# Retiming the pieces of a DFT inside a feed-forward token loop: inverse pieces five steps later, smaller first blocks, and a new plan for the second and third batches

## The chip, the cores and the metric

One core of one Trainium2 chip runs the whole kernel. The metric is the time of one execution on the device in microseconds, lower is better. A run without the profiler gives one time; a profiled execution gives a time too, and the span that its trace covers.

## The reference

The input `x` is 8 batches of 3008 tokens with 256 features. Each batch goes through a global filter along its tokens, and the result through a feed-forward layer with a PReLU whose negative slope is one number per hidden unit:

```python
X = np.fft.rfft(x, axis=1)
y = np.fft.irfft(X * (filt_r + 1j * filt_i)[None], n=3008, axis=1)
h = y.reshape(24064, 256) @ w_in                 # 256 -> 2048
g = np.maximum(h, 0.0) + alpha * np.minimum(h, 0.0)
out = g @ w_out                                  # 2048 -> 256
```

## The kernel before

**The transform.** 3008 is 47 times 64, so the forward and the inverse transform are each two sets of small matrix products in fp16 with a transposition between them. For one batch (`class Fft`) there are four kinds of pieces, each a few matmuls into one PSUM bank of the pool `psF`, which has two buffers:

- `piece_a` (16 of them; matmul in line 168): one matmul of 512 columns out of a loaded chunk `xs` of the input, evicted to `asb`. Every fourth is followed by `save_a` (L173), a DMA of a quarter of `asb` to DRAM. After all of them `turn_a` (L180) reads the whole back in another order, as `at`, in four DMAs of 384 KB.
- `piece_b` (12; L188): two matmuls of 256 columns out of `at`. VectorE multiplies the bank twice with the filter, into `uu` (L191) and `ww` (L192), two tiles of the pool `p_uw`.
- `piece_c` (12; L220 and L221): four matmuls of 256 columns out of `uu` and `ww`, evicted by ScalarE to `v`. Every third is followed by `turn_c` (L230), four DMAs of `v` to DRAM; after the last the whole is read back as `zt` (L236).
- `piece_d` (16; L243): four matmuls of 94 columns out of `zt`, evicted into `yT`, the transposed activations that the feed-forward layer reads. `yT` holds two batches.

Evictions are one helper each: ScalarE in line 250, VectorE in line 253. The input is loaded by GpSimd's queue (`load_x`, L123) into four chunk buffers: a chunk of the next batch can be loaded when the four pieces A of this batch that read it are done.

**The feed-forward layer.** The tokens of two batches at a time are cut into blocks (12 blocks of 512 tokens, one of them 384). A block has 16 steps, one for each 128 hidden units. In a step `up` issues two matmuls as wide as the block (L332); every second step ScalarE evicts two such results at once to `gt` (L337), and VectorE makes the PReLU of them with two multiplications (`m`, L340) and one addition (L341). In the same step `down` issues the second product for the block before this one: as many matmuls of 256 columns as that block has 128-token groups (L350). Results go out through `osb` (L355) and SyncE's queue (L316).

**The order.** It is written out by hand. The whole runs as one sequence of steps, 96 for a batch, and `plan` says which pieces follow the `up` and `down` of which step; `plan_fft` enters a batch's pieces. Every engine works through its instructions in the order of this plan, and SyncE's queue too: it holds the stores of results, `save_a`, `turn_a`, `turn_c` and the reads of `zt` in one line, and an entry that waits holds up all behind it. The first batch's transform runs ahead of step 0, apart from its last twelve pieces D. The second batch's pieces lie in the first batch's steps, and so on: each batch's A, B and C must be done, and its D begun, before the step in which its own tokens are reached.

Of the kernel before, what the change touches and what calls it, by code (L numbers as in the profile page):

```python
# [13 lines left out]
NFFT = 3008  # L14
# [52 lines left out]
def kernel(  # L67
# [17 lines left out]
    konst = ctx.enter_context(tc.tile_pool(name="konst", bufs=1))  # L85
    p_x = ctx.enter_context(tc.tile_pool(name="p_x", bufs=4))
    p_fft = ctx.enter_context(tc.tile_pool(name="p_fft", bufs=1))
    p_uw = ctx.enter_context(tc.tile_pool(name="p_uw", bufs=2))
    p_gt = ctx.enter_context(tc.tile_pool(name="p_gt", bufs=17))
    p_m = ctx.enter_context(tc.tile_pool(name="p_m", bufs=2))  # L90
    p_osb = ctx.enter_context(tc.tile_pool(name="p_osb", bufs=3))
# [28 lines left out]
    def load_x(b, c):  # L120
        xs = p_x.tile([2 * N1, 8 * D], FP16, name="xs")
        for h in range(2):
            nc.gpsimd.dma_start(out=xs[h * N1 : h * N1 + N1], in_=xrow(b, h, c))  # L123
        return xs
# [130 lines left out]
    both = (on_act, on_dve)  # L255
# [41 lines left out]
        f0.piece_d(i, both[i % 2], i % 2 == 1)  # L297


    sizes = [512] * 5 + [384] + [512] * 6  # L300
    blocks = []
    for p in range(NB // 2):
        t = 0
        for n, tn in enumerate(sizes):
            blocks.append((p, t, tn, 2 * p + (n >= 6)))
            t += tn

    def store(p, t0, osb, lane):
# [52 lines left out]
    def put(step, fn, *args):  # L361
        plan.setdefault(step, []).append((fn, args))

    def plan_fft(b, a0, ga, ta, b0, gap, d0):
        f = Fft(b)
        for i in range(16):
            put(a0 + ga * i, f.piece_a, i, on_act)
        for c in range(4):
            put(a0 + ga * (4 * c + 3), f.save_a, c)
            if b + 1 < NB:  # L370
                put(a0 + ga * (4 * c + 3) + 1,
                    lambda b=b, c=c: xc.update({(b + 1, c): load_x(b + 1, c)}))
        put(ta, f.turn_a, nc.sync)
        for kp in range(12):
            put(b0 + gap * kp, f.piece_b, kp)
            put(b0 + gap * kp + 3, f.piece_c, kp, on_act)
        for q in range(4):
            put(b0 + gap * (3 * q + 2) + 4, f.turn_c, q)
        for i in range(16):
            put(d0 + min(i, 4) + 2 * max(i - 4, 0), f.piece_d, i, on_act)  # L380

    for i in range(4, 16):
        put(i - 4, f0.piece_d, i, both[i % 2])
    plan_fft(1, 10, 1, 26, 40, 3, 92)
    plan_fft(2, 50, 2, 86, 104, 5, 187)
    for b in range(3, NB):
        p = 96 * (b - 1)
        plan_fft(b, p - 54, 2, p - 22, p + 6, 5, p + 91)

    prev = None  # L390
    step = 0
    for p, t0, tn, _ in blocks:
        blk = Block(p, t0, tn)
        for j in range(16):
            blk.up(j)
            if prev is not None:
                prev.down(j)
            for fn, args in plan.pop(step, ()):
                fn(*args)
            step += 1  # L400
        prev = blk
# [33 lines left out]
```

## Time and the profile before

| | us |
|---|---|
| times of three runs | 860.27, 862.39, 858.70 |
| median | 860.27 |
| profiled execution, own time | 863.19 |
| its span | 861.4 |
| TensorE busy in it | 799.4 (93%) |
| VectorE busy | 612.9 (71%) |
| ScalarE busy | 586.6 (68%) |

TensorE's matmuls overlap in the trace, so the mean duration of one (273 ns for 256 columns) is longer than the distance between two. "Granted clock" or PEclk is the TensorE clock as a share of full speed. An idle time is put down to what ended it. Step 0 starts 64.62 us into the span; what lies ahead of it is not touched by the change.

### The profile page before, as it was taken

To read this page: it belongs to the slowest core of one execution; us is meant where nothing else is said; L and a number is where in the kernel's file an instruction comes from. 1 tells how busy PE (TensorE), PEld (TensorE's weight loads), DVE (VectorE), ACT (ScalarE), POOL (GpSimd) and SP (SyncE) were. 2 spreads that over 40 slices of the span, in tenths; PEclk is the share of its full clock that TensorE was granted. 3 is DMA by queue.
4 is the path that set the end of the run, shared out by engine and by line. 5 is a ranking of instruction groups with operands and counts; after the bars stand their busy time and mean duration, and the time that the engine had idled before them with its cause. 6 is when DMAs were issued, how large, how long until landed. Compare 5 with 4: busy or idle time off the path is not lost.

```text
span 861.4 us, 15404 instructions
## 1 busy us (share of the span) xinstructions
PE 799.4 (93%) x5809; PEld 541.7 (63%) x5809; DVE 612.9 (71%) x1361; ACT 586.6 (68%) x817; POOL 41.4 (5%) x85
## 2 busy tenths in 40 slices
PE   3458989979999999999999999999999999999997
PEld 1134556756666766676666766676666766676665
DVE  2246668758877787678877787778877788777773
ACT  2027757767787767777777767777777866677663
POOL 4103000000000000000000000000000000000000
PEclk9989989999999999999999999999999999999999
DMA  9989835761368224772268323682148122411111
GB/s 212 250 171 197 179 69 133 157 144 41 75 148 199 60 62 97 172 158 51 53 162 195 73 64 83 164 181 50 43 120 186 50 68 50 129 38 39 39 41 49
DMA packets 95378, 95.95 MB, mean 111 GB/s; under 512 B 8312, under 2 KB 85128, under 8 KB 95176
## 3 DMA queue, kind: packets, MB, share of 16 engines
q1 hardware_dynamic: 85448, 78.19, 35.8%
q0 software_dynamic: 8256, 16.00, 12.3%
q10 hardware_dynamic: 1600, 0.79, 0.5%
q8 instruction: 45, 0.74, 0.4%
q14 instruction: 29, 0.24, 0.1%
HBM read 59.55 MB, written 49.81 MB: 127 GB/s over the span
## 4 chain that ended last, share of the span: by engine, by line
PE 70%; DVE 13%; ACT 7%; DMA 6%; issue 2%; SPq 1%; POOL 0%; ACTq 0%; DVEq 0%; POOLq 0%
PE hps L332 29%; PE op L350 28%; ACT gt L337 6%; DVE gt L341 4%; DVE m L340 4%; PE psF L168 3%; DVE ww L192 3%; DVE uu L191 3%; PE psF L221 2%; DMA at<-a_dram 2%; PE psF L243 2%; DMA a_dram<-asb 2%; PE psF L220 1%; DMA xs<-in_x_dram 1%; PE psF L188 1%
## 5 line engine op out<-in xcount | busy, mean ns | idle before, releaser
L337 ACT ACTIVATE gt<-hps 128x1024 f16<-128x1024 f32 (+1 forms) x384 | 385.1, 1003 | 134.6 <-PE hps L332 134.1
L332 PE MATMUL hps<-yT,win_s 128*128 128x512 f16 (+1 forms) x1536 | 454.3, 377 | 1.1 <-ACT yT L250 1.0
L350 PE MATMUL op<-wout_s,gt 128*128 128x256 f16 x3008 | 453.3, 273 | 0.6 <-DVE gt L341 0.6
L350 PEld LDWEIGHTS <-gt 128*128 128x128 f16 x3008 | 294.4, 98 | 192.5 <-issue 2.8
L340 DVE TENSOR_SCALAR m<-gt,alm_s 128x512 f16<-128x512 f16 (+1 forms) x768 | 233.5, 346 | 164.1 <-ACT gt L337 162.8
L341 DVE TENSOR_TENSOR gt<-gt,m 128x1024 f16<-128x1024 f16 (+1 forms) x384 | 261.6, 681 | 24.3 <-DVE m L340 0.9
L332 PEld LDWEIGHTS <-win_s 128*128 128x128 f16 x1536 | 145.6, 98 | 31.6 <-issue 5.0
L250 ACT ACTIVATE asb<-psF 96x512 f16<-96x512 f32 x120 | 70.7, 593 | 40.2 <-PE psF L168 40.2
L250 ACT ACTIVATE v<-psF 128x512 f16<-128x512 f32 x84 | 50.2, 598 | 34.9 <-PE psF L221 34.9
L250 ACT ACTIVATE yT<-psF 128x376 f16<-128x376 f32 x120 | 58.1, 484 | 20.9 <-PE psF L243 20.7
L191 DVE TENSOR_TENSOR uu<-psF,filt_s 128x512 f16<-128x512 f32 x84 | 57.4, 683 | 6.7 <-PE psF L188 6.7
L355 ACT ACTIVATE osb<-op 128x512 f32<-128x512 f32 x96 | 56.3, 587 | 6.9 <-PE op L350 3.7
L168 PE MATMUL psF<-xs,wf_s 94*96 94x512 f16 x120 | 47.8, 398 | 11.0 <-DMA xs<-in_x_dram 8.3
L192 DVE TENSOR_TENSOR ww<-psF,filts_s 128x512 f16<-128x512 f32 x84 | 57.1, 679 | 0.0
L123 POOL DMA_DIRECT2D xs<-in_x_dram x64 | 32.9, 522 | 458.2 <-PE psF L168 457.1
L243 PE MATMUL psF<-wi_s,zt 96*128 96x94 f16 x504 | 42.7, 207 | 10.8 <-DMA zt<-v_dram 9.0
L243 PEld LDWEIGHTS <-zt 96*128 96x128 f16 x512 | 36.3, 100 | 18.9 <-DMA zt<-v_dram 9.3
L221 PE MATMUL psF<-ww,twi_s 128*128 128x256 f16 x168 | 41.1, 272 | 6.2 <-DVE ww L192 3.5
L220 PE MATMUL psF<-uu,twi_s 128*128 128x256 f16 x168 | 42.9, 272 | 1.1 <-ACT yT L250 0.5
L188 PE MATMUL psF<-at,twf_s 128*128 128x256 f16 x168 | 32.3, 274 | 8.1 <-issue 4.5
L220 PEld LDWEIGHTS <-twi_s 128*128 128x128 f16 x192 | 19.0, 99 | 18.0 <-issue 13.2
L250 ACT ACTIVATE v<-op 128x512 f16<-128x512 f32 x12 | 7.2, 597 | 32.4 <-PE op L221 32.4
(35 smaller groups left out, 130.8 us busy)
## 6 DMA issues: line engine op xcount, KB each, us to landing
out_dram<-osb SPq DMA_DIRECT2D x128, 128.0 KB
a_dram<-asb SPq DMA_DIRECT2D x32, 384.0 KB
v_dram<-v SPq DMA_DIRECT2D x128, 96.0 KB
zt<-v_dram SPq DMA_DIRECT2D x32, 384.0 KB
xs<-in_x_dram POOLq DMA_DIRECT2D x64, 188.0 KB, 5.1
at<-a_dram SPq DMA_DIRECT2D x28, 384.0 KB
twi_s<-c_twi SPq DMA_DIRECT2D x2, 768.0 KB
filts_s<-filt_s SPq DMA_DIRECT2D x2, 768.0 KB
```

Source lines behind the costliest of these rows:

```text
L168: nc.tensor.matmul(ps[0:96], wf1_s, xs[:, o : o + 512], start=True, stop=True)
L191: nc.vector.tensor_mul(uu, px, filt_s[:, 2 * kp : 2 * kp + 2])
L192: nc.vector.tensor_mul(ww, px, filts_s[:, 2 * kp : 2 * kp + 2])
L220: nc.tensor.matmul(pv[:, kh], twi_s[:, k1, 0], uu[:, kh], start=True, stop=False)
L221: nc.tensor.matmul(pv[:, kh], twi_s[:, k1, 1], ww[:, kh], start=False, stop=True)
L243: nc.tensor.matmul(ps[:, m], self.zt[:, 8 * g + 4 * mh + m, dh * 128 : dh * 128 + 128], wi3_s, start=True, stop=True)
L250: nc.scalar.activation(o, i, AF.Copy)
L332: nc.tensor.matmul(self.hps[:, j % 2, 0:tn], win_s[:, kt, j * 128 : (j + 1) * 128], yT[:, kt, self.t0 : self.t0 + tn], start=(kt == 0), st ...
L337: nc.scalar.activation(g[:, :, 0:tn], self.hps[:, :, 0:tn], AF.Copy)
L340: nc.vector.tensor_scalar(m[:, i, 0:tn], g[:, i, 0:tn], 0.0, a, OP.min, OP.mult)
L341: nc.vector.tensor_add(g[:, :, 0:tn], g[:, :, 0:tn], m[:, :, 0:tn])
L350: nc.tensor.matmul(self.op[:, si % 2], self.gts[k][:, 128 * si : 128 * si + 128], wout_s[:, k], start=(k == 0), stop=(k == 15))
```

## The change

Six things change in the plan; no piece is added, and one block more is cut.

1. In batches 3 to 8 piece C follows its piece B by five steps instead of three, and so lands in the same step as the next piece B. `p_uw` gets three buffers instead of two.
2. The first pair of batches is cut into blocks of 256, 256, 384 and ten of 512 tokens: 13 blocks, so that the second batch begins at step 112 and all later ones 16 steps later than before.
3. The second batch's pieces A are spread over steps 18 to 48, one in two steps, and evicted by ScalarE and VectorE in turn (before: steps 10 to 25, one a step, all by ScalarE). Its `turn_a` is at step 49, its B from 62 and C from 65, one in three steps, D from 110.
4. The third batch's loads stand at step 52 in the plan, its pieces A at 69 to 99, its `turn_a` at 101, B from 118, C from 123.
5. From the fourth batch on, B begins one step earlier against the batch's start.
6. Pieces D begin with two in a step: two, two, one, and then one in two steps.

```diff
-    p_uw = ctx.enter_context(tc.tile_pool(name="p_uw", bufs=2))
+    p_uw = ctx.enter_context(tc.tile_pool(name="p_uw", bufs=3))
...
-    sizes = [512] * 5 + [384] + [512] * 6
-    blocks = []
+    blocks, begin = [], {}
     for p in range(NB // 2):
         t = 0
-        for n, tn in enumerate(sizes):
-            blocks.append((p, t, tn, 2 * p + (n >= 6)))
+        for tn in [256, 256, 384] + [512] * 10 if p == 0 else [512] * 5 + [384] + [512] * 6:
+            for half in range(2):
+                if t <= half * NFFT < t + tn:
+                    begin[2 * p + half] = 16 * len(blocks)
+            blocks.append((p, t, tn))
             t += tn
...
-    def plan_fft(b, a0, ga, ta, b0, gap, d0):
+    def plan_fft(b, a0, ga, ta, b0, gap, late, d0, x0, evict_a):
         f = Fft(b)
         for i in range(16):
-            put(a0 + ga * i, f.piece_a, i, on_act)
+            put(a0 + ga * i, f.piece_a, i, evict_a[i % 2])
         for c in range(4):
             put(a0 + ga * (4 * c + 3), f.save_a, c)
             if b + 1 < NB:
-                put(a0 + ga * (4 * c + 3) + 1,
+                put(max(x0, a0 + ga * (4 * c + 3) + 1),
                     lambda b=b, c=c: xc.update({(b + 1, c): load_x(b + 1, c)}))
         put(ta, f.turn_a, nc.sync)
         for kp in range(12):
             put(b0 + gap * kp, f.piece_b, kp)
-            put(b0 + gap * kp + 3, f.piece_c, kp, on_act)
+            put(b0 + gap * kp + late, f.piece_c, kp, on_act)
         for q in range(4):
-            put(b0 + gap * (3 * q + 2) + 4, f.turn_c, q)
+            put(b0 + gap * (3 * q + 2) + late + 1, f.turn_c, q)
         for i in range(16):
-            put(d0 + min(i, 4) + 2 * max(i - 4, 0), f.piece_d, i, on_act)
+            put(d0 + (i // 2 if i < 4 else 2 * i - 6), f.piece_d, i, on_act)
...
-    plan_fft(1, 10, 1, 26, 40, 3, 92)
-    plan_fft(2, 50, 2, 86, 104, 5, 187)
+    p = begin[1]
+    plan_fft(1, 18, 2, 49, p - 50, 3, 3, p - 2, p - 60, both)
+    plan_fft(2, p - 43, 2, p - 11, p + 6, 5, 5, begin[2] - 5, 0, (on_act, on_act))
     for b in range(3, NB):
-        p = 96 * (b - 1)
-        plan_fft(b, p - 54, 2, p - 22, p + 6, 5, p + 91)
+        p = begin[b - 1]
+        plan_fft(b, p - 54, 2, p - 22, p + 5, 5, 5, begin[b] - 5, 0, (on_act, on_act))
```

In `plan_fft` the batches count from 0: `plan_fft(1, ...)` is the second batch.

More of the change, by code (lines that the diff above doesn't have):

```diff
@@ L375, in plan_fft @@
             put(b0 + gap * kp, f.piece_b, kp)
-            put(b0 + gap * kp + 3, f.piece_c, kp, on_act)
+            put(b0 + gap * kp + late, f.piece_c, kp, on_act)
         for q in range(4):
-            put(b0 + gap * (3 * q + 2) + 4, f.turn_c, q)
+            put(b0 + gap * (3 * q + 2) + late + 1, f.turn_c, q)
         for i in range(16):
-            put(d0 + min(i, 4) + 2 * max(i - 4, 0), f.piece_d, i, on_act)
+            put(d0 + (i // 2 if i < 4 else 2 * i - 6), f.piece_d, i, on_act)
     for i in range(4, 16):
         put(i - 4, f0.piece_d, i, both[i % 2])
-    plan_fft(1, 10, 1, 26, 40, 3, 92)
-    plan_fft(2, 50, 2, 86, 104, 5, 187)
+    p = begin[1]
+    plan_fft(1, 18, 2, 49, p - 50, 3, 3, p - 2, p - 60, both)
+    plan_fft(2, p - 43, 2, p - 11, p + 6, 5, 5, begin[2] - 5, 0, (on_act, on_act))
     for b in range(3, NB):
-        p = 96 * (b - 1)
-        plan_fft(b, p - 54, 2, p - 22, p + 6, 5, p + 91)
+        p = begin[b - 1]
+        plan_fft(b, p - 54, 2, p - 22, p + 5, 5, 5, begin[b] - 5, 0, (on_act, on_act))
     prev = None
     step = 0
-    for p, t0, tn, _ in blocks:
+    for p, t0, tn in blocks:
         blk = Block(p, t0, tn)
```

## The prediction

> **What bounds the kernel now.** I read the busy shares by stage first. The columns: stretch and its length, busy time of TensorE, its weight loads, VectorE, ScalarE and GpSimd, then granted clock, DMA share and GB/s.
>
> ```profile
> 64.60:105.70 41.10, 37.84 (x246) 22.01 (x246) 28.11 (x65) 31.71 (x46) 8.59 (x17) 0.96 0.92 188
> 105.70:110.40 4.70, 0.21 (x3) 0.07 (x2) 1.27 (x3) 0.42 (x1) 0.00 (x0) 0.84 1.20 219
> 110.40:115.90 5.50, 5.50 (x21) 2.95 (x22) 2.60 (x5) 1.67 (x2) 0.00 (x0) 0.52 0.09 30
> 115.90:182.90 67.00, 63.97 (x480) 44.93 (x478) 50.84 (x113) 50.09 (x74) 4.01 (x8) 1.00 0.60 133
> 182.90:186.60 3.70, 0.08 (x2) 0.08 (x2) 1.18 (x3) 0.48 (x1) 0.00 (x0) 1.00 1.00 224
> 186.60:190.90 4.30, 4.30 (x22) 2.48 (x23) 2.60 (x5) 2.37 (x4) 0.00 (x0) 0.60 0.01 3
> 190.90:862.00 671.10, 657.73 (x4892) 455.54 (x4889) 504.69 (x1135) 485.87 (x670) 16.28 (x32) 1.00 0.40 95
> ```
>
> From 190.9 on TensorE is busy for 98%: every wait it has there is lost. Ahead of that it stands still twice, and works at half clock after each. The waits name both:
>
> ```profile
> PE psF L188 <- issue: 4.5, 1, 4.5
> PE psF L188 <- DMA at<-a_dram: 3.6, 1, 3.6
> PE psF L168 <- ACT v L250: 2.0, 5, 0.5
> ```
>
> Both stalls are the first B of a batch waiting for `at`. SyncE's queue shows the chain behind each:
>
> ```profile
> 94.01 0.31 SPq L173 DMA_DIRECT2D a_dram<-asb  x1
> 100.29 2.46 SPq L180 DMA_DIRECT2D at<-a_dram  x4
> ...
> 158.62 1.80 SPq L230 DMA_DIRECT2D v_dram<-v  x4
> 163.86 1.72 SPq L236 DMA_DIRECT2D zt<-v_dram  x4
> 165.63 2.35 SPq L316 DMA_DIRECT2D out_dram<-osb  x3
> 168.02 0.58 SPq L173 DMA_DIRECT2D a_dram<-asb  x1
> 175.64 4.06 SPq L180 DMA_DIRECT2D at<-a_dram  x4
> ```
>
> The last save of batch 2 takes 6.3 us (94.01 to 100.29), the reread 10.1 (to the first B at 110.36). For batch 3 the same queue carries the older batch's v, zt and three stores first, and the first B starts at 186.55.
>
> The small waits are in the groups of instructions (the number ahead of the arrow is the idle time just before them):
>
> ```profile
> L221 PE MATMUL psF<-ww,twi_s 128*128 128x256 f16 x168 | 41.1, 272 | 6.2 <-DVE ww L192 3.5
> L220 PE MATMUL psF<-uu,twi_s 128*128 128x256 f16 x168 | 42.9, 272 | 1.1 <-ACT yT L250 0.5
> ```
>
> Piece C waits for the filter products for 6.2 + 1.1 = 7.3 us in all, about 1.2 a batch.
>
> **C five steps late: gain 7.3, then what is next.** `ww` is done within three steps of its B, so at five steps the wait is gone: −7.3 (certain to a microsecond). But C now shares a step with the next B, and where the older batch's D or the next batch's A falls there too, three pieces want two `psF` banks, and the third waits for an eviction. Before shows the price, at step 52, where C, B and A meet:
>
> ```profile
> 126.24 0.38 PE L188 MATMUL psF<-at,twf_s 128*128 128x256 f16 x2
> 127.09 0.38 PE L168 MATMUL psF<-xs,wf_s 94*96 94x512 f16 x1 [0.47 <-ACT v L250]
> ```
>
> Counting such steps in the new plan (p is the step in which the batch before begins, from which `plan_fft` counts):
> - C, B, A: at p+50 and p+60 of each of five batches (158 and 168 for batch 3), even steps like 52: 10 × 0.47 = 4.7.
> - D, C, B: at p+15 of batches 4 to 8, odd steps, in which ScalarE first evicts `gt` (1.02). The first bank is free about 2.0 us into the step and TensorE wants it at 0.87 + 0.17 + 0.44 = 1.5: 5 × 0.55 = 2.8; once in batch 3 in an even step: 0.2.
> - Batch 2 beside A of batch 3 has four such steps now (2.0 in the waits above), and five after, on odd steps (about 0.62): +1.1.
> - Two D a step, the second pair behind the first's evictions: about 0.2 in each of six batches: 1.2.
>
> Sum 10.0 − 7.3 = **+2.7**. Bounds: the third piece may wait only the 0.17 that is left of the 2.0 after four waits of 0.47, and the D pairs nothing (−4.5), or all of it a quarter more (+5.2). I take the middle, since the step-52 row is the same arrangement.
>
> **Small blocks and spread pieces A: where batch 2's `at` starts.** VectorE's rows by width:
>
> ```profile
> L341 DVE TENSOR_TENSOR gt<-gt,m 128x1024 f16<-128x1024 f16 x352 | 243.7, 692 | 20.6 <-DVE m L340 0.9 <-PE hps L332 0.5
> L340 DVE TENSOR_SCALAR m<-gt,alm_s 128x512 f16<-128x512 f16 x704 | 216.0, 349 | 153.0 <-ACT gt L337 151.7
> L341 DVE TENSOR_TENSOR gt<-gt,m 128x768 f16<-128x768 f16 x32 | 17.8, 558 | 3.6 <-PE hps L332 0.5
> L340 DVE TENSOR_SCALAR m<-gt,alm_s 128x384 f16<-128x384 f16 x64 | 17.6, 317 | 11.1 <-ACT gt L337 11.1
> ```
>
> Two `m` overlap: two steps' PReLU takes 0.62 + 0.69 = 1.31 at 512 tokens and 0.55 + 0.56 = 1.11 at 384, so I take 0.91 at 256: half the tokens, but 70% of the time. TensorE needs 0.85 for such two steps, and 1.09 at 384: in the first 48 steps VectorE is the bound. It has six pairs of steps with a `yT` cast (0.91 + 0.5), ten without (0.91), eight of 384 (1.11) and eight `asb` casts (0.6, a little under their 687 ns): 8.5 + 9.1 + 8.9 + 4.8 = 31.3 us. Its first `m`, at 68.17 before, starts 1.3 sooner with narrower matmuls and evictions: 66.9, so the last A is evicted at 98.2. Save and reread take 0.1 + 6.3 + 10.1: B at **114.7**. TensorE reaches the last A (step 48) two pairs and a cast ahead of VectorE, about 95.9, and 14 steps of 0.76 (two up, three down) later, at 106.5, it wants that B: a stall of 8.2 us instead of 4.7. By then it has 4352 columns more behind it than before (44,032 against 41,984 of `up`, 27,904 against 25,600 of `down`), 1.8 us at 0.43 per 1024. So the loss is 114.7 − (110.36 + 1.8) = **+2.5**. Ends: A15 bound by TensorE alone (about 96.5) with a faster save, −0.5; the slower save and reread of batch 3's chain (7.6 and 10.9), +4.6.
>
> One rule decides otherwise. The Trainium skill ("DMA: Bandwidth & Descriptors", Anatomy of one DMA) puts a DMA at about 2 us plus its bytes at 436 GB/s, fitted on GpSimd's path; by that, an estimate, save and reread take 2.9 + 5.6 = 8.5 us, B starts at 106.8 and this stall is gone. The queue's rows say 16.4, and I go by them.
>
> **Batch 3's `at`.** Its last A now stands in step 99, the step of batch 2's last `turn_c` (before: three steps later). From the start of the last C to the first B the chain took 157.5 to 186.55, 29.0 us. Of it the three stores between zt and save go (2.4): 26.6. Cover: the C, 20 steps of 0.87, one A, eight D of 0.17 and the up matmul that waits for D as before (1.0): 0.4 + 17.4 + 0.2 + 1.4 + 1.0 = 20.4. A stall of 6.2 against 3.7: **+2.5** (ends: chain 25.0 to 29.0, so +0.9 to +4.9). D of batch 2, at step 110, has 11 steps instead of 15 after its `turn_c`; should it wait (0 to 2.3), that time comes off the stall behind it.
>
> **Half clock.** Before: 5.5 us at 0.52 cost 2.6, 4.3 at 0.60 cost 1.7. Both stalls get longer: 3.0 and 2.6, **+1.3** (0 to +3.7, if the first is like the start, where the clock came back 10.9 us after a wait of 17.9). The skill's page "TensorE: Matmul & The Clock Gate" (Part 1) speaks against longer stalls too: an idle window of about 3.4 us halves the clock until a busy one has passed.
>
> **Nothing:** the third `uu`/`ww` buffer (C comes ahead of B in its step, two suffice); the loads at step 52 (GpSimd's queue holds only loads there, which wait for pieces A, not steps); B one step earlier in later batches (their `at` is not waited for); 16 more steps of ScalarE evictions (68% busy).
>
> **Sum:** 2.7 + 2.5 + 2.5 + 1.3 = +9.0 on the profiled execution's 863.19 (span 861.4 and 1.8 around it): 872.2. The median of the runs is 2.9 lower: **869.2**.
>
> **Rivals.**
> - *Covered*: spread pieces A leave the DMA engines free (their share was 0.92 up to 105.7), and both `at` land in time. Then B starts at 106.5 (−5.7 instead of +2.5), 2.6 of half clock go, the second stall and its half clock go (−3.7 − 1.7), and 2.7 stay: −11, about 849. It decides if save and reread take under 8.3 us instead of 16.4. Against it: the reread took 10.1 us with only a few stores beside it. Chance 0.1.
> - *Cancelled*: the three-piece waits mostly don't arise (−4.5), against +6.3 for the rest: +1.8, about 862. For it: one of the five waits before was only 0.17. Chance 0.2.
> - *Slower*, the sum above: 0.7; with the upper ends it reaches 878.
>
> **Range.** All low ends together give −4 (856), all high ends +18 (878). I take 857 to 878; a tenth lies below. Faster by over 0.5%: 0.1; within 0.5% (856 to 864.6; about what a measurement can tell): 0.2; slower: 0.7.
>
> **What would show it.** Right: TensorE waits of 6 to 9 us before the first B of batch 2 (near 115) and 5 to 8 before batch 3's; VectorE nearly without idle from step 2 to 48; no wait for `ww`, and L168 and L188 waiting for ScalarE's `v` and `yT` by about 1.5 us a batch. Wrong: save and reread under 12 us, or a VectorE idle for a tenth of the first 30 us, or those bank waits absent.

## The result and the profile after

The changed kernel took 868.24 us (median of six runs, 865.36 to 870.32), the kernel before 860.66: a ratio of 1.0088 [1.0062, 1.0115], 7.6 us slower. The forecast was 869.2. One run of a later repeat of the changed kernel (889.49 us) fell into a slower state of the chip and is left out of the repeat's median and ratio below. The profiled execution took 867.41 (span 865.6), 4.2 us more than the one of before. That pair understates the loss: step 0, whose head is the same in both kernels, came at 62.37 us after and at 64.62 before. Counted from step 0, the profiled pair differs by 6.5.

Busy shares by stage, in the columns of the prediction (times, TensorE, its weight loads, VectorE, ScalarE, GpSimd, clock, DMA share, GB/s):

```profile
63.40:105.70 42.30, 41.57 (x297) 29.21 (x294) 37.18 (x104) 31.03 (x48) 8.35 (x17) 0.86 0.83 178
105.70:112.70 7.00, 0.04 (x1) 0.00 (x0) 1.31 (x3) 0.02 (x1) 0.00 (x0) 0.75 1.11 184
112.70:118.00 5.30, 5.26 (x27) 3.21 (x28) 2.75 (x6) 2.52 (x4) 0.00 (x0) 0.69 0.12 29
118.00:182.00 64.00, 58.85 (x430) 40.29 (x427) 47.31 (x102) 46.76 (x67) 4.20 (x8) 1.00 0.57 127
182.00:187.50 5.50, 0.03 (x1) 0.00 (x1) 0.96 (x3) 0.48 (x1) 0.00 (x0) 0.70 1.21 211
187.50:194.60 7.10, 7.10 (x45) 4.51 (x46) 3.91 (x8) 4.10 (x6) 0.00 (x0) 0.75 0.22 62
194.60:866.00 671.40, 655.54 (x4892) 456.36 (x4889) 509.68 (x1135) 489.49 (x670) 16.08 (x32) 1.00 0.40 95
```

Both stalls are still there, and longer: 7.0 us (was 4.7) and 5.5 (was 3.7). The tail is as full as before, 98%. (The code grew by two lines ahead of the token loop: L332 of before is L334 here, L316 is L318.) The waits of TensorE, in us in total, times, and the longest:

```profile
PE psF L188 <- DMA at<-a_dram: 12.5, 2, 7.0
PE psF L168 <- ACT v L250: 8.9, 19, 1.0
PE psF L188 <- ACT yT L250: 4.5, 5, 0.9
```

The first line is the two stalls. The other two are third pieces that wait for a bank of `psF`: 13.4 us, where before had 2.0 in one line and none in the other. What they replace is gone without rest, as the groups of piece C show (the last number is idle time):

```profile
L220 PE MATMUL psF<-uu,twi_s 128*128 128x256 f16 x168 | 41.3, 273 | 0.0
L221 PE MATMUL psF<-ww,twi_s 128*128 128x256 f16 x168 | 41.2, 272 | 0.0
```

SyncE's queue ahead of the two stalls (start, duration of the issue):

```profile
95.43 2.12 SPq L318 DMA_DIRECT2D out_dram<-osb  x3
97.65 0.52 SPq L173 DMA_DIRECT2D a_dram<-asb  x1
102.24 2.08 SPq L180 DMA_DIRECT2D at<-a_dram  x4
...
162.07 1.79 SPq L230 DMA_DIRECT2D v_dram<-v  x4
168.12 1.72 SPq L236 DMA_DIRECT2D zt<-v_dram  x4
169.89 0.42 SPq L173 DMA_DIRECT2D a_dram<-asb  x1
177.46 2.42 SPq L180 DMA_DIRECT2D at<-a_dram  x4
```

Batch 2's last save takes 4.6 us (97.65 to 102.24) and the reread 10.5 (to the first B at 112.73). Batch 3's chain runs 25.4 us from the `v` stores to its B at 187.50, where before took 27.9: 2.5 less, which is the 2.4 of the three stores that no longer stand in it.

The loss by stretch, each against before and less the change in matmul columns (at the prediction's 0.43 us per 1024): step 0 to batch 2's first B went from 45.74 to 50.36 us with 1.8 us more work, a loss of 2.8; from there to batch 3's first B from 76.19 to 74.77 with 4.4 less work, a loss of 3.0; from there to the last `up` from 661.48 to 664.76 with 2.6 more work, a loss of 0.7. The sum is 6.5, the profiled pair's difference from step 0 on.

### The profile page after: what moved, and what is told of

It reads as the page before. It is cut to its first block, busy times and chain, and to the rows that moved or that the text cites. A ratio compares the mean times of both kernels' runs of the same rounds, so it can differ in the third digit from the quotient of the medians.

```text
span 865.6 us, 15510 instructions
## 1 busy us (share of the span) xinstructions
PE 797.9 (92%) x5841; PEld 547.4 (63%) x5841; DVE 625.2 (72%) x1393; ACT 588.6 (68%) x817; POOL 41.1 (5%) x85
## 4 chain that ended last, share of the span: by engine, by line
PE 82%; DMA 7%; ACT 4%; DVE 3%; issue 2%; SPq 1%; POOL 0%; ACTq 0%; DVEq 0%; POOLq 0%
PE op L352 35%; PE hps L334 35%; DMA at<-a_dram 3%; PE psF L168 3%; PE psF L243 2%; DMA a_dram<-asb 2%; PE psF L188 2%; PE psF L221 2%; PE psF L220 2%; ACT v L250 1%; ACT gt L339 1%; DMA xs<-in_x_dram 1%; DVE m L342 1%; DVE gt L343 1%; ACT yT L250 1%
## 5 line engine op out<-in xcount | busy, mean ns | idle before, releaser
L339 ACT ACTIVATE gt<-hps 128x1024 f16<-128x1024 f32 (+2 forms) x392 | 386.7, 986 | 150.8 <-PE hps L334 136.6
L334 PE MATMUL hps<-yT,win_s 128*128 128x512 f16 (+2 forms) x1568 | 458.4, 375 | 1.9 <-ACT yT L250 1.5
L342 DVE TENSOR_SCALAR m<-gt,alm_s 128x512 f16<-128x512 f16 (+2 forms) x784 | 236.5, 344 | 154.5 <-ACT gt L339 153.2
L343 DVE TENSOR_TENSOR gt<-gt,m 128x1024 f16<-128x1024 f16 (+2 forms) x392 | 262.8, 670 | 23.3
L334 PEld LDWEIGHTS <-win_s 128*128 128x128 f16 x1568 | 150.1, 99 | 39.8 <-issue 12.5
L250 ACT ACTIVATE asb<-psF 96x512 f16<-96x512 f32 x112 | 66.3, 592 | 42.8 <-PE psF L168 42.8
L188 PE MATMUL psF<-at,twf_s 128*128 128x256 f16 x168 | 32.5, 275 | 17.2 <-DMA at<-a_dram 12.5
L221 PE MATMUL psF<-ww,twi_s 128*128 128x256 f16 x168 | 41.2, 272 | 0.0
L188 PEld LDWEIGHTS <-twf_s 128*128 128x128 f16 x168 | 16.0, 98 | 20.5 <-issue 13.2
```

What stands on the lines that cost most here:

```text
L188: nc.tensor.matmul(px[:, kh], twf_s[:, k1], self.at[:, k1], start=True, stop=True)
L221: nc.tensor.matmul(pv[:, kh], twi_s[:, k1, 1], ww[:, kh], start=False, stop=True)
L250: nc.scalar.activation(o, i, AF.Copy)
L334: nc.tensor.matmul(self.hps[:, j % 2, 0:tn], win_s[:, kt, j * 128 : (j + 1) * 128], yT[:, kt, self.t0 : self.t0 + tn], start=(kt == 0), st ...
L339: nc.scalar.activation(g[:, :, 0:tn], self.hps[:, :, 0:tn], AF.Copy)
L342: nc.vector.tensor_scalar(m[:, i, 0:tn], g[:, i, 0:tn], 0.0, a, OP.min, OP.mult)
```

## The experiments

The theory going in was the prediction's: bank waits eat the gain at C, and two later `at` make the loss. Edits are on the kernel before or on the changed one, as said; `plan_fft` counts batches from 0. Each kernel's ratio is to the kernel before, run on the same chip. Where a gain against the changed kernel is given in us, it is a difference of medians from different chips, on which the kernel before read 860.66 to 861.68, so it holds to about 1 us.

**The steady part alone** (before, with C five steps late and its `turn_c` with it from batch 3 on, two D in a step, B one step earlier from batch 4 on; `p_uw` with three buffers):

```diff
...
-            put(b0 + gap * kp + 3, f.piece_c, kp, on_act)
+            put(b0 + gap * kp + (5 if b > 1 else 3), f.piece_c, kp, on_act)
...
-            put(d0 + min(i, 4) + 2 * max(i - 4, 0), f.piece_d, i, on_act)
+            put(d0 + (i // 2 if i < 4 else 2 * i - 6), f.piece_d, i, on_act)
...
-        plan_fft(b, p - 54, 2, p - 22, p + 6, 5, p + 91)
+        plan_fft(b, p - 54, 2, p - 22, p + 5, 5, p + 91)
```

> The kernel before with only the steady part of the change (C five steps late, D two in a step at first, B one step earlier from batch 4 on); blocks and the plan of batches 2 and 3 up to its B as before. My theory: the waits for ww go, three-piece steps come instead, and the two about cancel: +0.5 to +3 us against before, no wait of TensorE for ww in the waits, about 4.5 us of B waiting for a yT eviction and 5 us of A waiting for a v eviction. Rival (the five steps are the gain that the change was after, and the loss is all in front): 5 to 8 us faster than before.

Measured: 861.82 us, ratio 1.0010 [0.9990, 1.0031]. No wait of the transform's pieces for `ww` in the token loop is left. In its place:

```profile
PE psF L168 <- ACT v L250: 7.6, 20, 0.5
PE psF L188 <- ACT yT L250: 4.5, 5, 0.9
```

Five steps of distance trade one wait for another, and gain nothing. The rival falls.

**Four steps instead of five** (before, C of batches 3 to 8 and its `turn_c` alone moved, `p_uw` with three buffers; `late` is 4; no step then holds three pieces for that reason):

```diff
...
-            put(b0 + gap * kp + 3, f.piece_c, kp, on_act)
+            put(b0 + gap * kp + (late if b > 1 else 3), f.piece_c, kp, on_act)
```

> The kernel before with C four steps behind B from batch 3 on, and nothing else (the pool uw with three buffers). C then stands one step ahead of the next B, so that no step holds three pieces. My theory (what eats the gain of the later C is the sharing of two psF banks within one step, not the lateness): no wait for ww, hardly any for v or yT after batch 2, 6 to 12 us faster than before. Rival (a later C delays its evictions and the turn behind it whatever the step): no faster than before, within 2 us.

Measured: 850.73 us, ratio 0.9887 [0.9845, 0.9929], 10 us faster. The waits:

```profile
PE psF L168 <- ACT v L250: 2.9, 10, 0.5
```

L221's idle is 0.0 here too, and these 2.9 us of bank waits stand where five steps of distance had 12.1 (7.6 and 4.5). So the wait for `ww` was worth removing. These two kernels differ in D and in B's step as well; that the fifth step is what spoils it is shown by the change of C alone, below.

**The small blocks alone** (before, with every piece of batches 2 to 8 sixteen steps later, as the first blocks make 16 more):

```diff
...
-        for n, tn in enumerate(sizes):
-            blocks.append((p, t, tn, 2 * p + (n >= 6)))
+        for tn in [256, 256, 384] + [512] * 10 if p == 0 else [512] * 5 + [384] + [512] * 6:
+            blocks.append((p, t, tn, 0))
...
-    plan_fft(1, 10, 1, 26, 40, 3, 92)
-    plan_fft(2, 50, 2, 86, 104, 5, 187)
+    plan_fft(1, 26, 1, 42, 56, 3, 108)
+    plan_fft(2, 66, 2, 102, 120, 5, 203)
...
-        p = 96 * (b - 1)
+        p = 96 * (b - 1) + 16
```

> The kernel before with only the first blocks of 256, 256 and 384 tokens, and every piece of batches 2 to 8 put 16 steps later, so that it keeps its place against its batch's start. My theory: VectorE bounds the first 48 steps but carries no asb evictions here, so the last A is done about 25 us after step 0 and the first B of batch 2 starts about 41 us after it (before 45.7), with 2.7 us less of matmul columns behind it: 0 to 3 us faster than before; the loss of the change's front is then in its late pieces A, not in the small blocks. Rival (VectorE's fixed cost on half-size tiles makes the small blocks themselves the loss): 2 to 4 us slower than before.

Measured: 860.11 us, ratio 0.9978 [0.9960, 0.9996]: 1.9 faster by the ratio. Inside, the reading was off: the last A began 29.0 us after step 0 where I had it done by 25, and batch 2's B 46.88 where I had 41, with a stall of 7.4; in exchange batch 3 had no stall at all. The blocks alone are not what costs.

**Batch 2's A packed, one a step** (changed kernel):

```diff
-    plan_fft(1, 18, 2, 49, p - 50, 3, 3, p - 2, p - 60, both)
+    plan_fft(1, 16, 1, 33, p - 50, 3, 3, p - 2, p - 60, both)
```

> The changed kernel with batch 2's pieces A in steps 16 to 31, one in each, and its at reread at step 33, all else as in it. My theory (the first stall is the chain from the last A's eviction through save and reread, 15.6 us, against a cover of 14 steps): with 30 steps of cover the 7.0 us wait before the first B of batch 2 is gone and half clock after it too: 5 to 9 us faster than the changed kernel, so about 859 to 863, and step 62 is reached up to 2 us later than at 105.7 because the eight VectorE evictions still lie ahead of it. Rival (VectorE is the bound up to there, so the wait only turns into others): under 2 us faster than the changed kernel.

Measured: 863.67 us, 4.6 under the changed kernel, just short of what I expected. Batch 2's B no longer waits; one wait for `at` is left, the second stall:

```profile
PE psF L188 <- DMA at<-a_dram: 5.0, 1, 5.0
```

But the first A now waits 2.9 us for its input, with 3.4 us of half clock behind that wait in place of those behind the first stall, and six others wait 0.24 us each for evictions.

**C four steps late** from batch 3 on (changed kernel):

```diff
-    plan_fft(2, p - 43, 2, p - 11, p + 6, 5, 5, begin[2] - 5, 0, (on_act, on_act))
+    plan_fft(2, p - 43, 2, p - 11, p + 6, 5, 4, begin[2] - 5, 0, (on_act, on_act))
...
-        plan_fft(b, p - 54, 2, p - 22, p + 5, 5, 5, begin[b] - 5, 0, (on_act, on_act))
+        plan_fft(b, p - 54, 2, p - 22, p + 5, 5, 4, begin[b] - 5, 0, (on_act, on_act))
```

> The changed kernel with C four steps behind B from batch 3 on instead of five; blocks, batch 2 and the D spacing as in it. My theory (in the changed kernel, too, the shared step is what costs: every wait of B for yT and the waits of A for v in batches 4 to 8 come from it): these waits go, 7 to 11 us faster than the changed kernel, 857 to 861. Rival (the other parts of the plan, two D in a step and the earlier B, bring waits of their own): under 4 us faster.

Measured: 855.78 us, ratio 0.9935 [0.9917, 0.9953]: 12.5 under the changed kernel, more than I expected, and 5 under before.

```profile
PE psF L168 <- ACT v L250: 3.7, 6, 1.0
```

The 4.5 us behind `yT` are gone, and 5.2 of the 8.9 behind `v`: 9.7 of the 12.5. They were 18 waits, and the part of a wait that the trace doesn't show, 0.16 us each (below), makes 2.9 of them: 12.6 in all. Here C alone moved, so the fifth step's cost is shown.

**Batch 3's A six steps earlier** (changed kernel):

```diff
-    plan_fft(2, p - 43, 2, p - 11, p + 6, 5, 5, begin[2] - 5, 0, (on_act, on_act))
+    plan_fft(2, p - 49, 2, p - 11, p + 6, 5, 5, begin[2] - 5, 0, (on_act, on_act))
```

> The changed kernel with batch 3's pieces A six steps earlier (63 to 93 instead of 69 to 99), its reread at step 101 as before: the last save is then out before the last turn of batch 2. Two readings of the 5.5 us wait before batch 3's first B. Chain of latencies (v, zt, save, reread one behind the other): without the save the wait falls by its 7.5 us to nothing, 4 to 7 us faster than the changed kernel. DMA throughput (zt and at are 1.6 MB each and take about 10 us each, the save is done only 1 us after zt): the wait falls by 1 to 3 us, and so the time by 1 to 3 us. I expect the second.

Measured: 860.87 us, ratio 0.9993 [0.9978, 1.0009]: 7.4 under the changed kernel, and level with before. The second stall fell from 5.47 to 0.66 us (of the 7.6 below, 6.9 is the first stall), with no half clock behind it. The wait and the queue:

```profile
PE psF L188 <- DMA at<-a_dram: 7.6, 2, 6.9
...
162.70 1.79 SPq L230 DMA_DIRECT2D v_dram<-v  x4
166.16 1.72 SPq L236 DMA_DIRECT2D zt<-v_dram  x4
167.92 6.66 SPq L180 DMA_DIRECT2D at<-a_dram  x4
```

With the last A ahead of the last C, no save stands between `zt` and `at`, so the reread is issued at 167.92 instead of 177.46, and B starts at 183.10 instead of 187.50 (counted from step 0, 10.5 and 5.4 us earlier). I had put more weight on the DMA engines being full, and had 1 to 3 us for it: the save's place in the queue was worth more than that. The engines count too: right behind `zt` the reread takes 15.2 us from its issue to B, where it took 10.0 behind the save.

**The best of these together** (changed kernel's blocks; C four steps late everywhere; D one a step as before; batch 2's A at one a step; batch 3's A well ahead):

```diff
-            put(d0 + (i // 2 if i < 4 else 2 * i - 6), f.piece_d, i, on_act)
+            put(d0 + min(i, 4) + 2 * max(i - 4, 0), f.piece_d, i, on_act)
...
-    plan_fft(1, 18, 2, 49, p - 50, 3, 3, p - 2, p - 60, both)
-    plan_fft(2, p - 43, 2, p - 11, p + 6, 5, 5, begin[2] - 5, 0, (on_act, on_act))
+    plan_fft(1, 18, 1, 35, p - 56, 3, 4, p - 4, 0, (on_act, on_act))
+    plan_fft(2, p - 60, 2, p - 13, p + 12, 5, 4, begin[2] - 5, 0, (on_act, on_act))
...
-        plan_fft(b, p - 54, 2, p - 22, p + 5, 5, 5, begin[b] - 5, 0, (on_act, on_act))
+        plan_fft(b, p - 54, 2, p - 22, p + 6, 5, 4, begin[b] - 5, 0, (on_act, on_act))
```

> What the runs so far point to, in the blocks of the change: C four steps behind B in every batch, one D a step at first, batch 2's pieces A in steps 18 to 33 by ScalarE and its B from step 56, batch 3's A in steps 52 to 82 and its B from 124. By the sum: 7 to 11 us for the late C, 5 for the first stall, 5 to 7 for the second and its half clock off the changed kernel's 868: 845 to 852, level with or faster than the kernel before with C four steps late (850.7). Rival (work gained in front is lost to VectorE's bound and the transfers run into each other): 853 or more.

Measured: 844.55 us, ratio 0.9809 [0.9787, 0.9831]. It beats both kernels. Against the changed one it gains 23.7; the three single edits gave 4.6, 12.5 and 7.4, together 24.5 (by the ratios 24 against 27). Batch 2's B still waits for 3.9 us.

**Who sets the first stall: VectorE?** (changed kernel, batch 2's A evicted by ScalarE alone):

```diff
-    plan_fft(1, 18, 2, 49, p - 50, 3, 3, p - 2, p - 60, both)
+    plan_fft(1, 18, 2, 49, p - 50, 3, 3, p - 2, p - 60, (on_act, on_act))
```

> The changed kernel with all of batch 2's pieces A evicted by ScalarE. My theory (VectorE bounds the first 48 steps, its last eviction of an A ends 34.8 us after step 0 and the reread hangs on it): without its eight evictions (about 4.8 us) TensorE's own pace bounds, the last A is evicted 2 to 3.5 us sooner, the first B of batch 2 starts 2 to 3.5 us sooner, and the time is 2 to 3.5 us less than the changed kernel's. Rival (the chain is set by TensorE and DMA, VectorE has slack): within 1 us of the changed kernel, or slower, as ScalarE gets the work.

Measured: 866.03 us, ratio 1.0058 [1.0031, 1.0084]. That is a lower ratio than the changed kernel's, but on another chip, with overlapping intervals, and in its profile TensorE waited 2.65 us for an input at the first A, so it decided nothing. (Half clock ended 4.1 us after step 0 there, against 12.6 in the changed kernel's profile, so TensorE reached that A 1.8 us sooner; the input was not there yet.) I ran the pair again side by side, the changed kernel first:

> The changed kernel once more, on the same chip as the next kernel, for a comparison of these two alone: 866 to 870.

> The changed kernel with all of batch 2's pieces A evicted by ScalarE, a second time: in the first profile the input came 2.7 us late, which hid the effect. In the changed kernel the last A waits 2.4 us from its matmul to the end of its eviction behind VectorE's queue, against 1.2 us on ScalarE. If VectorE's queue sets when the reread starts: 1 to 3 us faster than the changed kernel beside it. If the input's arrival or TensorE's pace sets it: within 1 us.

Measured: 867.30 us (five runs) and 868.37 us (six), ratios 1.0073 [1.0049, 1.0097] and 1.0071 [1.0047, 1.0096]. By the ratios the two are 0.2 us apart: taking A's evictions off VectorE buys nothing that can be measured. The intervals, some 2 us to either side, would still hide a gain of 1 us or 2; what decides is SyncE's queue in the second:

```profile
96.24 2.11 SPq L318 DMA_DIRECT2D out_dram<-osb  x3
98.45 0.53 SPq L173 DMA_DIRECT2D a_dram<-asb  x1
```

The last eviction ended 33.4 us after step 0, 1.4 earlier than in the changed kernel's first profile (34.8). But the save stands behind three stores of results and went out 35.2 us after step 0, against 35.3.

## Why the prediction was right

The sign, the size and the two places were right; of the terms, several were off, in opposite directions, so that the sum came so close is partly luck.

- **C's wait for `ww`.** Gone, as predicted. (Of the 7.3, 0.5 was for `yT` by the prediction's own line, but that went too.)
- **C, B, A.** Predicted 10 × 0.47. Measured exactly 0.47 at all ten steps, and 0.17 at four more: 5.4 against 4.7. The row of before at step 52 was the right one to take.
- **D, C, B.** Predicted 0.55 at five steps; measured 0.93, 0.83, 0.93, 0.83 and 0.93. The step that failed is the count of ScalarE's work ahead of the bank: I let it evict `gt` alone first. The first of these steps (start, duration, what; in brackets the wait):

```profile
297.77 1.02 ACT L339 ACTIVATE gt<-hps 128x1024 f16<-128x1024 f32 x1 [0.51 <-PE hps L334]
298.69 0.59 ACT L357 ACTIVATE osb<-op 128x512 f32<-128x512 f32 x1
299.17 0.49 ACT L250 ACTIVATE yT<-psF 128x376 f16<-128x376 f32 x1
...
299.71 0.38 PE L188 MATMUL psF<-at,twf_s 128*128 128x256 f16 x2 [0.93 <-ACT yT L250]
```

An `osb` eviction of 0.59 us stands between `gt` and `yT`, and in the 0.83 steps one of 0.38. Such a step is priced by all that its evicting engine has queued, not by the one operation in view.

- **Batch 2 beside A of batch 3.** Predicted +1.1. The waits are 1.00, 0.51, 0.51, 0.51, 1.00 and 0.12 where before had 2.0: +1.6. The `up` of step 112 that waits for `yT` costs 1.5 instead of 1.0, which I had left at its old price.
- **Two D in a step.** Predicted 1.2 in all. No such wait shows; the term was put in without a row of before that showed it, and was wrong.
- **The first stall.** Predicted 8.2 with B 50.1 us after step 0; measured 7.0 with B at 50.4, a loss of 2.8 against 2.5. The number held, the cause did not, and it held by luck: the last save went out 1.6 us later than predicted (35.3 against 33.7), and save and reread took 15.1 instead of 16.4. VectorE worked 29.5 us between its first `m` and its last `asb` cast, which ended 34.8 us after step 0 (31.3 and 33.6 predicted). It was idle for 4.7 of the first 30 us after step 0, 16%: more than the tenth that the prediction had named as a sign of being wrong. And with A off VectorE the save goes out at the same time. TensorE, busy for 41.57 of the 42.30 us and at half clock until 12.6 us after step 0, reaches the last A 32.4 us after step 0 with VectorE's evictions and 32.2 without (31.3 by the prediction), and then SyncE's queue, with three stores in front, sets the save. The step that failed is "in the first 48 steps VectorE is the bound". How much of the loss of 2.8 is the late clock (before, half clock ended 3.3 us after step 0) was not isolated.
- **The second stall.** Predicted 6.2 from a chain shortened by the stores' 2.4; measured 5.5 and a chain shortened by 2.5. The third experiment on the changed kernel shows the mechanism: take the save out of the chain and the stall is down to 0.7, with 7.4 us gained.
- **Half clock.** Predicted +1.3 because the stalls are longer; wrong in sign. Clock states in the trace come in stretches of 3.4 us. Before, they lie at 108.91 to 115.74 and 187.41 to 190.82, so that 5.4 us of the first and all 3.4 of the second fell on work (batch 3's B began at 186.55, still at full clock). After, they lie at 109.13 to 115.96 and 184.23 to 191.06, and 3.2 and 3.6 us fell on work. At half speed that is (8.8 − 6.8) / 2, some 1.0 us less lost. In these four, how much of a stretch falls on work goes by where the stall ends in it, not by the stall's length: the longest stall, 7.0 us, has the shortest rest.

The terms that came out larger (D, C, B by 1.6; C, B, A by 0.7; batch 2 and the `up` by 1.1; the first stall by 0.3: 3.7) and those that came out smaller (half clock by 2.3, D pairs by 1.2, the second stall by 0.7: 4.2) nearly cancel. The profile's idle times have a bias besides: a 256-column matmul lasts 273 ns in the trace, while in a running stream the next starts 109 ns after it. If a wait breaks the stream, it costs the difference, 0.16 us, more than the idle time shown. This can be tested on a steady batch, the 96 steps of batch 3's tokens: from the changed kernel to C four steps late they shrank from 98.54 to 95.87 us, 2.67; the idle shown is 2.04 in four waits, and with 4 × 0.164 that makes 2.70. It holds for before against its version with four steps too: 97.69 to 96.33, 1.36 measured; 0.72 shown and four waits fewer, 1.38. In the batch after that it is 2.56 against 2.59, and 1.92 against 2.06. So the 7.3 us of `ww` waits cost more than 7.3, the new waits more than 13.4, and the steady part came out near zero in the experiment where the page's idle times alone would have it some 3 us slower.

On the two rivals. *Covered* asked for save and reread under 8.3 us; they took 15.1. The Trainium skill ("DMA: Bandwidth & Descriptors", Anatomy of one DMA) would have put them, by estimate, at 8.5; its fit is for a single DMA on GpSimd's path, and here four of 384 KB go out together behind a save, and the stretch's DMA share reads 1.11. Which of these makes the difference no run here shows. *Cancelled* asked for bank waits that mostly don't arise; the first experiment shows them nearly all.

What stays open: the loss left over when the steady part (+0.9 by its ratio) and the blocks (−1.9) are taken from the whole (+7.6) is 8.6 us, and it would belong to the new plans of batches 2 and 3. Moving batch 3's A alone takes back 7.4, packing batch 2's A alone 4.6: together more than the 8.6, since each stall changes what follows it (with the blocks alone batch 3's stall was gone, and batch 2's longer). The shares of the two plans were not separated further.

## What to carry to other kernels

A distance between a producer and a consumer should clear the wait and no more: four steps removed the wait for 10 us, the fifth put the consumer into the same step as the next producer, where three users met two banks, and gave all of it back. When a plan moves work earlier or later, follow it through the queue that carries its DMA: the save behind `zt` made the second stall, and the stores ahead of the save took back what faster evictions gave to the first; VectorE, on which I had put that stall, did not set it. Price a shared step by everything that the evicting engine has queued in it, and add the 0.16 us of each wait that the profile's idle time leaves out.

## What was not expected of the hardware

The clock at the start of the token loop. The changed kernel, and the kernel with batch 2's A packed, over their first 12.5 us of steps (same columns; the eighth is the clock):

```profile
62.40:75.00 12.60, 11.62 (x81) 8.31 (x82) 8.78 (x26) 6.81 (x14) 4.31 (x9) 0.50 1.03 216
...
63.60:76.00 12.40, 8.97 (x84) 6.33 (x84) 9.85 (x31) 7.08 (x15) 4.29 (x9) 0.84 1.02 218
```

The first 12 steps are the same in both. In the first the clock stays at half for all 12.6 us, though TensorE is busy for 92% of them; in the second it is back after 4 us. Half clock lasted to 74 to 76 us in five of the profiles with these steps and to 66 to 68 in three, and step 12 came 10.8 us after step 0 in the former, 9.3 to 9.4 in the latter: 1.5 us of scatter between kernels whose first 12 steps are the same. In the three profiles whose first block has 512 tokens half clock ended 3.3 to 4.4 us after step 0; whether the small blocks make the late end more frequent was not tested.

The Trainium skill ("TensorE: Matmul & The Clock Gate", Part 1) says that one sustained busy window of about 3.4 us restores the clock. The traces show stretches of the same 3.4 us. On that grid the changed kernel has these windows up to the clock's return at 75.00 (stretch and length, TensorE's busy time, clock, DMA share, GB/s):

```profile
61.35:64.76 3.41, 3.05 (x28) 0.50 1.09 267
64.76:68.17 3.41, 3.12 (x25) 0.50 0.97 184
68.17:71.59 3.42, 3.13 (x26) 0.50 0.96 205
71.59:75.00 3.41, 3.26 (x21) 0.50 1.05 210
```

The first three are 89% to 92% busy and half clock goes on after each; after the fourth, 96%, it ends. In the kernel with A packed the grid lies otherwise against step 0: its first whole window, 64.21 to 67.62, is 96% busy already, and half clock ends with it. So where step 0 falls in the grid seems to decide. The busy share alone does not: in the first run with A's evictions all on ScalarE a window 88% busy (78.25 to 81.66) was enough.
